# An attention and two-layer MLP kernel on one core: first transfers in the order of use, and a new written order of the first group's work

## The chip, the core and the metric

One core of a Trainium2 chip runs the whole kernel. The metric is the device time of one execution in microseconds (us); lower is better. The core has five engines that run side by side, each with its own queue in program order: the Tensor engine (PE in the profile, its weight loads PEld), the Vector engine (DVE), the Scalar engine (ACT), GpSimd (POOL) and SyncE (SP), which here does nothing but issue transfers.

## The reference

Three stages in a row. The first is an attention over 32 learned slots; batch 4, 8 heads, 576 tokens, head width 64:

```python
a = softmax(phi, axis=tokens)                      # per head and slot
k_m = a.T @ k;  v_m = a.T @ v                      # 32 x 64 per head
attn = softmax(q @ k_m.T / 8, axis=slots)
x = (attn @ v_m)                                   # 2304 tokens x 512
h = x @ w_in;  x2 = max(0.01 * h, h) @ w_out       # 512 -> 2048 -> 512
# then: each token goes to the best two of 8 experts, 512 -> 1024 -> 512
```

The change touches the first two lines of work alone: how batch 0 and batch 1 of the attention and the first 512 columns of the two-layer MLP get started.

## The kernel before, in words

**Groups and slots.** The MLP runs in groups (batch, chunk c of 512 of the 2048 middle columns). A group has 8 slots: two token halves u of 288 tokens, times four blocks f of 128 middle columns. A slot n is a middle product (six matmuls, L587) with its leaky maximum, and an output product (four column blocks of three matmuls, L625) that accumulates in PSUM over the four f of a half. From slot 8 on a loop plans the work. The first group (slots 0 to 7, batch 0, chunk 0), together with all that must precede it, is written out by hand, as one string of 221 step names (L1038 to L1049), each of which issues its instructions on every engine's queue in that order; this string is one of the two places that the change rewrites.

**The steps' names.** A digit behind a name is a batch, a half, a block or a slot.
- `mx`, `mt`, `mb`, `sb`, `ex`, `su`: phi of a batch: maximum over tokens (DVE, L331), its two transposes (PE, L338 and L346), subtraction (DVE, L352), exp (ACT, L356), sum (DVE, L361). `mx10` is batch 1, first half.
- `kk`, `kv`, `kb`: slot sums of k alone, v alone (batch 0) and both (batch 1) on PE (L379); `de`, `rd`, `no`, `kt`: denominator, reciprocal, normalizing on ACT (L399), transpose.
- `qa`, `qb`, `qc`: transposes of q (PE L368, ACT copy L370) for batch 0 first half, batch 0 second half, batch 1 first half. The steps beginning with `sa`, `sb`, `sc` are the softmax of the scores of the same three: scores (PE L416), transpose, maximum, subtraction, exp (ACT L436), sum, product, transpose back, and the split into a high and a low part (L457, L462).
- `c0` to `c7` with `a`, `h`, `s`, `l`, `o`: turning one 128 x 512 tile of 64-bit weights into 32-bit ones: one ACT pass (L204), three DVE passes (L210, L215, L220), and for tiles of the second layer (c4 to c7) the split into two parts (ACT L238, POOL L239). c0 to c3 are the first layer's tiles.
- `v0m`, `v0h`, `v0l`: v_m times the first layer's weights (PE L552) and its split (ACT L557, DVE L561). Every middle product needs all of it.
- `l0` to `l7` with `mm`, `sc`, `mx`, `hi`, `lo`: a slot's middle product (PE), scaled copy (ACT L593), maximum (DVE L598), split (ACT L603, POOL L608). `y20` is the output product of slot 2, column block 0.
- `Lqb`, `Lph`, `Lr6` and so on issue transfers.

**Buffers.** phi has one buffer; PSUM has four tiles of kind "y" (used by the start and by output products), two of kind "m", two of kind "h" (middle products).

**First transfers.** Before the string, SP issues phi, k of batch 0, two first-layer tiles, q, a third tile, v, the fourth tile and two tiles of the second layer (L255 to L273).

Of the kernel before, what the change touches and what calls it, by code (L numbers as in the profile page):

```python
# [20 lines left out]
def moe_kernel(  # L21
# [36 lines left out]
    NW, NRAW, NPOOL = 29, 4, 64  # L58
# [22 lines left out]
    def spare(s0, n, p=128):  # L81
        return big[:p, s0 * NDB * TU:s0 * NDB * TU + n]
# [85 lines left out]
    def load_q(b, u):  # L168
        if (b, u) == (1, 0):
            t = spare(2, HJ * H * D, P).rearrange("p (j h d) -> p j h d", j=HJ, h=H)  # L170
        else:
            t = att.tile([P, HJ, H, D], F32, name="q", bufs=1)
        for j in range(HJ):
            nc.sync.dma_start(t[:, j], q[b].rearrange("h (p j) d -> p j h d", j=J)[:, u * HJ + j])  # L174
        QR[b, u] = t
# [10 lines left out]
    def load_raw(n):  # L186
        if n >= len(items):
            return
        kind, a, db = items[n]
        if n in (NRAW, NRAW + 1):  # L190
            t = spare(6, 2048).bitcast(I32)[:, (n - NRAW) * 1024:(n - NRAW + 1) * 1024].rearrange("p (c t) -> p c t", t=2)
        else:
            t = conv.tile([128, 512, 2], I32, name="raw64", bufs=NRAW)
        if kind == "i":
            nc.sync.dma_start(t, w_in_w[db * 128:(db + 1) * 128, a * 512:(a + 1) * 512, :])  # L195
        else:
            nc.sync.dma_start(t, w_out_w[a * 128:(a + 1) * 128])
        RAW[n] = t
# [57 lines left out]
    kv0 = spare(0, 2 * H * J * D, P).rearrange("p (i h j d) -> p i h j d", i=2, h=H, j=J)  # L256
# [3 lines left out]
    def load_kv0(i):  # L260
        for s in range(2):
            nc.sync.dma_start(kv0[:, i, 4 * s:4 * s + 4].rearrange("p h j d -> p h (j d)"),
                              (k, v)[i][0, 4 * s:4 * s + 4].rearrange("h (p j) d -> p h (j d)", j=J))

    load_kv0(0)
    load_raw(0)
    load_raw(1)
    load_q(0, 0)
    load_raw(2)
    load_kv0(1)  # L270
    load_raw(3)
    load_raw(4)
    load_raw(5)  # L273


    jp = consts.tile([128, 128], I32)
# [759 lines left out]
    for c in range(3):  # L1036
        steps[f"Lk{c}"] = (load_kv, 1, c)
    order = """  # L1038
        mx00 mt00 mb00 mx01 sb00 ex00 mt01 mb01 sb01 ex01 kk0 su01 c1a kk1 kk2 su00 c1h dek c0a qa0 rdk nok qa1 qa2 ktk c1s
        c0h samm c2a Lqb c0s c0l Lr6 c2h kv0 kv1 kv2 Lph satr samx c4a c3a sasb saex c2s c2l nov qb0 qb1 ktv  # L1040
        c4h c1l Lr7 c3h c1o sasu c5a qb2 c3s samu sabk c2o sahi salo@g Lqc c0o v0m0 v0m1 c5h c5s mx10 c6a
        c3l c6h c5l mx11 c3o v0m2 v0m3 mt1 v0h0 v0l0 sbmm v0h1 v0l1 l0mm mb1 l1mm l0sc Lr8 sb10 ex10 sbtr c4s
        sb11 c4l c4o l1sc c7a sbmx l0mx l0hi l0lo sbsb qc0 l2mm l1mx l3mm y00 y01 c6s Lk0 c5o c7h l1hi l1lo sbex
        sbsu sbmu ex11 qc1 qc2 y02 l2sc l2mx l2hi y03 sbbk sbhi c6l su10 y10 y11 Lk1 Lk2 y12 kb0 kb1 kb2
        su11 deb l2lo Lr9 l3sc y13 c6o y20 l3mx l3hi l3lo y21 c7s c7l c7o y22 y23 sblo l4mm l5mm rdb nob
        l4sc l4mx l4hi l5sc l5mx l4lo y30 y31 ktb l6mm l6sc l6mx Lr10 y32 y33 scmm sctr y40 scmx y41 y42 y43
        l7mm l5hi l5lo v1m0 v1m1 v1m2 v1m3 Lr11 y50 y51 l7sc y52 scsb scex l6hi l7mx l7hi scsu scmu scbk
        schi l6lo sclo v1h0 y53 y60 l7lo v1h1 y61 y62 v1l0 y63 y70 y71 y72 v1l1 y73 Lqd
    """.split()  # L1049
    first = {"kk0", "kv0", "ktk", "ktv", "qa0", "qa1", "qa2", "samm", "v0m0", "mt00", "mt01", "mt1"}  # L1050
    engines = {"d": nc.vector, "g": nc.gpsimd}
# [227 lines left out]
```

## Time and profile before

| | us |
|---|---|
| median of 3 runs (921.24 to 923.18) | 921.34 |
| the profiled execution | 923.07 |
| its span, first to last instruction | 921.1 |
| PE busy in the span | 876.2 (95%) |
| DVE busy in the span | 544.0 (59%) |
| ACT busy | 355.9 (39%) |
| POOL busy | 194.3 (21%) |

The profiled execution is 1.73 us above the median, and 1.97 us of it lie around the span. Shares over the whole span are averages of stages with different limits, so the stage that the change touches (roughly the first 80 us) has to be read by itself: in the tables by stretch of time, in the list of who waited for whom, and in the instructions in order of time.

### The profile page before, as it was taken

The page shows a single profiled execution, that of the slowest core. Times are in us where ns is not written, and L with a number is a line of the kernel's source. Part 1 is how long each engine was busy: PE and PEld are TensorE (multiplying, and loading weights), DVE is VectorE, ACT ScalarE, POOL GpSimd, SP SyncE. Part 2 cuts the span into 40 slices and gives each one's busy share as a digit, 9 for nine tenths or more (in the row PEclk, how much of TensorE's full clock was granted, in tenths as well). Part 3 has the DMA queues.
Part 4 walks back from the last instruction along what each step waited for, and adds up shares of the span by engine and source line. Part 5 has one row for each costly group of instructions (what it writes and reads, how often), then busy time and mean ns, then how long its engine had stood idle before and what let it go on. Part 6 is the DMA issues. An engine that isn't in the chain of part 4 may idle for free.

```text
span 921.1 us, 16145 instructions
## 1 busy us (share of the span) xinstructions
PE 876.2 (95%) x6296; PEld 783.4 (85%) x6296; DVE 544.0 (59%) x1306; ACT 355.9 (39%) x784; POOL 194.3 (21%) x195
## 2 busy tenths in 40 slices
PE   4579999999999999999999999999999999999996
PEld 2377778999999998889888988998889888998895
DVE  5698988466666867878956544535444353442312
ACT  2346556545444544444624342333323332331110
POOL 0042224333200000000103320513215142130402
PEclk9999999999999999999999999999999999999998
DMA  8989723012431111212625543533434343230201
GB/s 208 256 178 192 187 73 93 1 46 74 172 145 46 35 59 50 75 43 82 203 78 186 186 148 114 190 104 129 145 113 169 125 146 139 98 122 1 82 22 57
DMA packets 82614, 105.29 MB, mean 114 GB/s; under 512 B 23988, under 2 KB 58836, under 8 KB 82528
## 3 DMA queue, kind: packets, MB, share of 16 engines
q1 hardware_dynamic: 70528, 71.58, 27.0%
q0 software_dynamic: 9312, 27.88, 9.1%
q10 hardware_dynamic: 2688, 4.72, 1.6%
q8 instruction: 51, 0.84, 0.4%
q14 instruction: 35, 0.29, 0.1%
HBM read 85.88 MB, written 19.53 MB: 114 GB/s over the span
## 4 chain that ended last, share of the span: by engine, by line
PE 82%; DVE 9%; DMA 3%; ACT 2%; SPq 2%; issue 1%; POOL 0%; POOLq 0%; DVEq 0%; ACTq 0%
PE py L881 24%; PE ph L863 23%; PE py L625 18%; PE ph L587 9%; PE pxt L838 2%; PE pvw L552 2%; PE pi L769 1%; DMA big<-in_moe_w_out_dram 1%; DMA row<-x,get 1%; DVE mx L361 1%; DVE wi L215 1%; SPq L195 1%; DVE mx L331 1%; SPq L174 1%; PE pg L653 1%
## 5 line engine op out<-in xcount | busy, mean ns | idle before, releaser
L863 PE MATMUL ph<-xh,w2l 128*128 128x256 f32 (+1 forms) x512 | 155.9, 305 | 0.0
L863 PE MATMUL ph<-xh,w2h 128*128 128x256 f32 (+1 forms) x512 | 155.7, 304 | 0.2 <-ACT xh L840 0.2
L625 PE MATMUL py<-gh,woh 128*128 128x288 f32 x512 | 154.8, 303 | 0.8 <-ACT big L632 0.6
L813 DVE TENSOR_TENSOR w2l<-r,w2h 128x512 fp32r<-128x512 f32 x128 | 87.6, 686 | 114.8 <-ACT w2h L812 54.0
L863 PE MATMUL ph<-xl,w2h 128*128 128x256 f32 (+1 forms) x512 | 155.3, 303 | 0.0
L625 PE MATMUL py<-gl,woh 128*128 128x288 f32 x512 | 153.1, 299 | 0.4 <-POOL gl L608 0.4
L625 PE MATMUL py<-gh,wol 128*128 128x288 f32 x512 | 151.6, 296 | 0.0
L881 PE MATMUL py<-w2h,gh 128*128 128x512 f32 (+1 forms) x320 | 129.4, 404 | 0.0
L812 ACT ACTIVATE w2h<-r 128x512 fp32r<-128x512 f32 x128 | 79.5, 628 | 123.3 <-PE py L881 94.1
L881 PE MATMUL py<-w2h,gl 128*128 128x512 f32 (+1 forms) x320 | 126.3, 395 | 0.0
L866 ACT ACTIVATE gh<-ph 128x256 fp32r<-128x256 f32 (+1 forms) x128 | 54.4, 425 | 186.1 <-PE ph L863 173.7
L881 PE MATMUL py<-w2l,gh 128*128 128x512 f32 (+1 forms) x320 | 126.2, 395 | 0.0
L867 DVE SCALAR_TENSOR_TENSOR gl<-ph,gh 128x256 fp32r<-128x256 f32 (+1 forms) x128 | 60.5, 473 | 99.9 <-ACT gh L866 92.6
L825 POOL DMA_INDIRECT row<-x,get x40 | 43.9, 1096 | 345.4 <-DVE put L776 228.6
L625 PEld LDWEIGHTS py<-gh,woh 128*128 128x128 f32 x512 | 96.5, 189 | 18.1 <-issue 15.7
L863 PEld LDWEIGHTS ph<-xh,w2h 128*128 128x128 f32 x512 | 96.5, 189 | 5.0 <-ACT xh L840 0.7
L625 PEld LDWEIGHTS py<-gl,woh 128*128 128x128 f32 x512 | 96.6, 189 | 3.6 <-issue 2.7
L863 PEld LDWEIGHTS ph<-xl,w2h 128*128 128x128 f32 x512 | 96.5, 188 | 3.3 <-DVE xl L841 0.2
L625 PEld LDWEIGHTS py<-gh,wol 128*128 128x128 f32 x512 | 96.8, 189 | 0.5 <-issue 0.5
L863 PEld LDWEIGHTS ph<-xh,w2l 128*128 128x128 f32 x512 | 96.4, 188 | 0.0
L598 DVE TENSOR_TENSOR sm<-ph,sm 128x288 f32<-128x288 f32 x128 | 57.5, 451 | 57.5 <-ACT sm L593 56.8
L608 POOL TENSOR_TENSOR gl<-sm,gh 128x288 fp32r<-128x288 f32 x64 | 59.2, 927 | 127.0 <-ACT gh L603 111.3
(164 smaller groups left out, 1507.8 us busy)
## 6 DMA issues: line engine op xcount, KB each, us to landing
r<-in_moe_w_dram SPq DMA_DIRECT2D x64, 512.0 KB, 3.7
raw<-in_moe_w_in_dram SPq DMA_DIRECT2D x16, 512.0 KB, 3.9
raw<-in_moe_w_out_dram SPq DMA_DIRECT2D x14, 512.0 KB, 4.2
out_dram<-zr SPq DMA_DIRECT2D x18, 256.0 KB, 3.0
x<-xr ACTq DMA_DIRECT2D x24, 192.0 KB, 2.1
q<-in_q_dram SPq DMA_DIRECT2D x21, 192.0 KB, 4.9
phi<-in_phi_dram SPq DMA_DIRECT2D x8, 288.0 KB, 3.1
kv<-in_k_dram SPq DMA_DIRECT2D x6, 384.0 KB, 6.3
```

The lines of the kernel that those rows point to most:

```text
L552: nc.tensor.matmul(VW[b, c][g][hp * M:(hp + 1) * M, :], VT[b][g * 64:(g + 1) * 64, 1, hp * M:(hp + 1) * M], WI[c, hp][g * 64:(g + 1) * 64, ...
L587: nc.tensor.matmul(ph, w_[:, o:o + 128], a_[:, g], start=(t == 0), stop=(t == 5))
L598: nc.vector.tensor_tensor(sm, ph, sm, op=OP.max)
L608: (eng or (nc.gpsimd if n < NPOOL else nc.vector)).tensor_sub(lo, sm, hi.bitcast(F32))
L625: nc.tensor.matmul(py, w_[:, s], g_, start=(first and i == 0), stop=(last and i == 2))
L812: nc.scalar.activation(h_, src, AF.Copy)
L813: nc.vector.tensor_sub(l_, src, h_.bitcast(F32))
L825: nc.gpsimd.indirect_dma_start(out=xg[:sz], out_offset=None, in_=x2[:(B - 1) * S] if (e, c) == (0, 0) else x2, in_offset=bass.IndirectOffs ...
L863: nc.tensor.matmul(ph[:, :n], w_[:, s], x_[:, db], start=(t == 0), stop=(t == 3 * NDB - 1))
L866: nc.scalar.activation(hi, ph[:, :n], AF.Relu)
L867: nc.vector.scalar_tensor_tensor(lo, ph[:, :n], 0.0, hi.bitcast(F32), op0=OP.max, op1=OP.subtract)
L881: nc.tensor.matmul(PY[c, t][:sz], h_[:, o:o + sz], w_, start=(f == 0 and i == 0), stop=(f == NF2 - 1 and i == 2))
```

## The change

It does two things. SP's first transfers come in another order: q ahead of the first weight tile, v right behind that tile, and the other tiles after v. And the string of steps is written anew: the same 221 names, none added or taken out. Output products stand right behind the middle products of their slots, the conversion of the second layer's tiles stands between them, and the work on phi of batch 1 (`mx10`, `mx11`, `mt1`, ...) stands behind the conversion of the last tile.

```diff
     load_kv0(0)
+    load_q(0, 0)
     load_raw(0)
-    load_raw(1)
-    load_q(0, 0)
-    load_raw(2)
     load_kv0(1)
-    load_raw(3)
-    load_raw(4)
-    load_raw(5)
+    for n in range(1, NRAW + 2):
+        load_raw(n)
...
-        c4h c1l Lr7 c3h c1o sasu c5a qb2 c3s samu sabk c2o sahi salo@g Lqc c0o v0m0 v0m1 c5h c5s mx10 c6a
...
+        sbex l2mx l2hi l2lo l3mm y00 y01 y02 y03 c6a c6h Lr8 l3sc l3mx l3hi l3lo sbsu sbmu c6s c6l c6o sbbk sbhi sblo
```

SP's queue, where the program starts; before:

```order
L151 DMA phi<-in_phi_dram 96x4x192 x2
L262 DMA big<-in_k_dram 96x4x384 x2
L195 DMA raw_87<-in_moe_w_in_dram 128x1024
L195 DMA raw_89<-in_moe_w_in_dram 128x1024
L174 DMA q<-in_q_dram 96x8x64 x3
L195 DMA raw_95<-in_moe_w_in_dram 128x1024
L262 DMA big<-in_v_dram 96x4x384 x2
L195 DMA raw_99<-in_moe_w_in_dram 128x1024
```

and with the change:

```order
L151 DMA phi<-in_phi_dram 96x4x192 x2
L262 DMA big<-in_k_dram 96x4x384 x2
L174 DMA q<-in_q_dram 96x8x64 x3
L195 DMA raw_91<-in_moe_w_in_dram 128x1024
L262 DMA big<-in_v_dram 96x4x384 x2
L195 DMA raw_95<-in_moe_w_in_dram 128x1024
L195 DMA raw_97<-in_moe_w_in_dram 128x1024
L195 DMA raw_99<-in_moe_w_in_dram 128x1024
```

v has moved ahead of three weight tiles; q has moved ahead of all.

DVE's queue around the first middle products, from the back transpose of the first softmax on; before (`mx<-phi` is the maximum over batch 1's phi, `vwl` the last thing that the middle products wait for):

```order
L451 STREAM_TRANSPOSE ar<-sx 128x576
L210 TENSOR_SCALAR wi<-wi 128x512
L215 SCALAR_TENSOR_TENSOR wi<-big,wi 128x512
L331 TENSOR_REDUCE mx<-phi 96x128
L220 SCALAR_TENSOR_TENSOR wi<-raw_99,wi 128x512
L210 TENSOR_SCALAR wi<-wi 128x512
L220 SCALAR_TENSOR_TENSOR wi<-big,wi 128x512
L331 TENSOR_REDUCE mx<-phi 96x128
L340 TENSOR_REDUCE cm<-pm 128x2
L561 TENSOR_TENSOR vwl<-pvw,vwh 128x512 x2
```

and with the change (line numbers are lower by three from here on):

```order
L448 STREAM_TRANSPOSE ar<-sx 128x576
L220 SCALAR_TENSOR_TENSOR wi<-raw_95,wi 128x512
L210 TENSOR_SCALAR wi<-wi 128x512
L215 SCALAR_TENSOR_TENSOR wi<-raw_97,wi 128x512
L220 SCALAR_TENSOR_TENSOR wi<-raw_97,wi 128x512
L210 TENSOR_SCALAR wi<-wi 128x512
L215 SCALAR_TENSOR_TENSOR wi<-raw_99,wi 128x512
L220 SCALAR_TENSOR_TENSOR wi<-raw_99,wi 128x512
L558 TENSOR_TENSOR vwl<-pvw,vwh 128x512 x2
```

Both maxima, the reduction of their transposes and five passes over second-layer tiles no longer stand ahead of `vwl`.

DVE's queue where those maxima now stand, behind the last pass over tile 7 (`raw_319`; `sm` is a slot's maximum, `ups` to `cnt` are constants for later):

```order
L220 SCALAR_TENSOR_TENSOR wi<-raw_319,wi 128x512
L328 TENSOR_REDUCE mx<-phi 96x128
L293 TENSOR_SCALAR ups<-jp 96x96
...
L595 TENSOR_TENSOR sm<-ph,sm 128x288
L328 TENSOR_REDUCE mx<-phi 96x128
...
L595 TENSOR_TENSOR sm<-ph,sm 128x288
L337 TENSOR_REDUCE cm<-pm 128x2
L349 TENSOR_TENSOR phi<-phi,pm 96x768 x2
L595 TENSOR_TENSOR sm<-ph,sm 128x288
L358 TENSOR_REDUCE mx<-phi 96x128 x2
L595 TENSOR_TENSOR sm<-ph,sm 128x288
```

From here on batch 1's maxima, subtractions and sums follow one another, with one slot maximum between them at a time.

## Rows read from the trace of the kernel before

**Rows 1.** Busy time of each engine by stretch; behind a stretch its length, (x) instructions.

```profile
0.00:22.60 22.60, 9.63 (x133) 6.57 (x133) 11.38 (x19) 6.80 (x12) 1.67 (x8) 1.00 0.85 207
22.60:43.60 21.00, 11.30 (x144) 5.78 (x144) 14.60 (x26) 6.61 (x14) 1.41 (x1) 1.00 1.05 259
43.60:81.80 38.20, 32.47 (x306) 28.72 (x299) 32.45 (x53) 18.12 (x43) 14.55 (x14) 1.00 0.95 197
81.80:155.00 73.20, 68.77 (x723) 59.33 (x722) 68.43 (x118) 45.19 (x105) 18.82 (x20) 1.00 0.49 123
155.00:438.00 283.00, 281.22 (x2225) 260.95 (x2224) 196.02 (x624) 131.64 (x308) 33.97 (x37) 1.00 0.21 70
```

**Rows 2.** In order of time: start, us, engine, line; in brackets idle before it.

```profile
12.97 2.78 PE L379 MATMUL pk<-big,phi 96*32 96x64 f32 x92 [2.06 <-DMA big<-in_k_dram]
...
26.88 2.78 PE L379 MATMUL pk<-big,phi 96*32 96x64 f32 x92 [2.24 <-DMA big<-in_v_dram]
...
37.69 1.44 DVE L331 TENSOR_REDUCE mx<-phi 96x128 f32<-96x768 f32 x1 [1.75 <-DMA phi<-in_phi_dram]
...
39.78 1.92 PE L552 MATMUL pvw<-wi,kvT 64*32 64x512 f32 x4 [3.50 <-DVE wi L220]
...
43.59 0.61 PE L587 MATMUL ph<-ah,vwh 128*128 128x288 f32 x1
...
80.52 1.28 DVE L561 TENSOR_TENSOR vwl<-pvw,vwh 128x512 fp32r<-128x512 f32 x2
```

**Rows 3.** DVE's waits, 43.6 to 81.8: in total, times, longest.

```profile
DVE sm L598 <- ACT sm L593: 2.7, 4, 0.8
DVE phi L352 <- PE pm L346: 1.8, 1, 1.8
```

**Rows 4.** By stretch, as rows 1; the last two columns are DMA share and GB/s.

```profile
15.50:19.50 4.00, 3.01 (x25) 2.57 (x17) 1.59 (x5) 2.11 (x6) 0.00 (x0) 1.00 0.49 119
19.50:30.00 10.50, 5.12 (x117) 3.33 (x115) 5.60 (x10) 2.65 (x7) 0.00 (x0) 1.00 1.08 298
```

**Rows 5.** By stretch, instructions on the softmax's tile sx alone: DVE busy, ACT busy.

```profile
22.50:34.40 11.90, 4.62 (x7) 0.67 (x1) 1.00 1.05 296
```

**Rows 6.** DVE in order of time: three conversion passes, and the softmax's start.

```profile
22.59 0.84 DVE L423 STREAM_TRANSPOSE sx<-psc 128x288 f32<-128x288 f32 x2
...
34.78 0.43 DVE L210 TENSOR_SCALAR wi<-wi 128x512 int32<-128x512 int32 x1 [0.46 <-ACT wi L204]
35.24 0.69 DVE L215 SCALAR_TENSOR_TENSOR wi<-big,wi 128x512 int32<-128x512 int32 x1
...
39.98 0.68 DVE L220 SCALAR_TENSOR_TENSOR wi<-big,wi 128x512 int32<-128x512 int32 x1
```

**Rows 7.** Groups of 0 to 85: busy us, mean ns, then idle before.

```profile
L370 ACT ACTIVATE qT<-pq 128x384 f32<-128x384 f32 x12 | 5.7, 495 | 3.9 <-PE pq L368 3.7
L204 ACT ACTIVATE wi<-raw 128x512 f32<-128x512 f32 x8 | 5.3, 671 | 8.0 <-DMA raw<-in_moe_w_in_dram 7.0 <-DMA raw<-in_moe_w_out_dram 1.0
L603 ACT ACTIVATE gh<-sm 128x288 fp32r<-128x288 f32 x9 | 3.9, 447 | 5.2 <-DVE sm L598 5.2
L593 ACT ACTIVATE sm<-ph 128x288 f32<-128x288 f32 x9 | 3.7, 411 | 5.1 <-PE ph L587 5.0
L238 ACT ACTIVATE woh<-wi 128x512 fp32r<-128x512 f32 x4 | 2.5, 631 | 3.7 <-DVE wi L220 3.7
```

**Rows 8.** PE in order of time, products of the same size (288 columns).

```profile
53.73 0.45 PE L625 MATMUL py<-gh,woh 128*128 128x288 f32 x1
53.98 0.45 PE L625 MATMUL py<-gl,woh 128*128 128x288 f32 x1
...
56.48 0.29 PE L625 MATMUL py<-gl,woh 128*128 128x288 f32 x1
56.60 0.29 PE L625 MATMUL py<-gh,wol 128*128 128x288 f32 x1
```

**Rows 9.** SP in order of time: phi of batch 2, issued once its buffer is free.

```profile
62.33 0.33 SPq L151 DMA_DIRECT2D phi<-in_phi_dram  x1
```

More of the change, by code (lines that the diff above doesn't have):

```diff
@@ L1038, in moe_kernel @@
     order = """
-        mx00 mt00 mb00 mx01 sb00 ex00 mt01 mb01 sb01 ex01 kk0 su01 c1a kk1 kk2 su00 c1h dek c0a qa0 rdk nok qa1 qa2 ktk c1s
-        c0h samm c2a Lqb c0s c0l Lr6 c2h kv0 kv1 kv2 Lph satr samx c4a c3a sasb saex c2s c2l nov qb0 qb1 ktv
-        c4h c1l Lr7 c3h c1o sasu c5a qb2 c3s samu sabk c2o sahi salo@g Lqc c0o v0m0 v0m1 c5h c5s mx10 c6a
[L1042 to L1048, printed above, removed]
+        mx00 mt00 mb00 mx01 sb00 ex00 mt01 mb01 sb01 ex01 kk0 su00 kk1 kk2 su01 dek qa0 c0a rdk nok qa1 qa2 ktk c0h c0s
+        c0l Lqb samm Lr6 satr samx c1a sasb saex kv0 kv1 kv2 Lph c1h c1s nov sasu c2a samu ktv sabk c1l Lr7 c2h c2s sahi
+        c0o c1o salo@g c3a c2l Lqc c3h c3s c3l c2o c3o v0m0 v0m1 v0m2 v0m3 v0h0 v0l0 v0h1 v0l1 c4a c4h qb0 qb1 l0mm
+        l1mm c4s l0sc c4l qb2 l0mx c4o l0hi l0lo c5a sbmm c5h l1sc c5s l1mx l1hi l1lo l2mm sbtr c5l c5o l2sc sbmx sbsb
+        sbex l2mx l2hi l2lo l3mm y00 y01 y02 y03 c6a c6h Lr8 l3sc l3mx l3hi l3lo sbsu sbmu c6s c6l c6o sbbk sbhi sblo
+        y10 y11 y12 y13 c7a c7h Lk0 c7s c7l c7o qc0 Lr9 y20 y21 y22 y23 l4mm l4sc mx10 l4mx l4hi l4lo qc1 qc2 Lk1 Lk2 l5mm
+        mx11 l5sc l5mx l5hi l5lo y30 y31 y32 y33 mt1 mb1 sb10 ex10 l6mm l6sc sb11 l6mx ex11 l6hi l6lo su10 Lr10
+        y40 y41 y42 y43 kb0 kb1 kb2 su11 deb l7mm l7sc l7mx l7hi l7lo rdb nob y50 y51 y52 ktb scmm sctr y53 scmx
+        y60 y61 Lr11 v1m0 v1m1 v1m2 v1m3 scsb scex y62 y63 v1h0 v1h1 scsu y70 v1l0 scmu scbk y71 schi v1l1 sclo y72 y73 Lqd
     """.split()
```

## The prediction

> **What bounds the kernel now.** I read the busy time by stretch first. From 155 us on PE is full (281.22 of the 283.00 us of the last stretch) and DVE is not; between 81.8 and 155 us both are close to full, 68.77 and 68.43 of 73.20 us [rows 1]. Nothing in those stretches is edited, so whatever the change does, it does by moving the moment at which slot 8 can start. That moment is 81.8 us, the end of the split of batch 1's v product: DVE's two instructions from 80.52 us [rows 2]. A shift of it goes through to the end, because the work behind it fills DVE and then PE and leaves no slack to take it up.
>
> So the first 81.8 us are the case. Here DVE is the fullest engine: 11.38, 14.60 and 32.45 us in the three stretches, together 58.43 us of work [rows 1]. The other 23.4 us it waits: 11.2 us up to 22.6, 6.4 us up to the first middle product at 43.59, and 5.75 us from there. The string names the same steps before and after, so DVE's 58.4 us stay. **The forecast is therefore a count of DVE's waits in the new order.**
>
> **Up to the first softmax.** The new transfer order closes a hole: between 15.5 and 19.5 us the DMA engines worked at a share of 0.49, against 1.08 right after [rows 4], that is (1.08 - 0.49) / 1.08 x 4 = 2.2 us of lost transfer. Batch 0's v, needed at 26.88 us before [rows 2], gets those 2.2 us and the time of two tiles of 0.52 MB that no longer precede it, 3.5 us at 298 GB/s [rows 4]: it should land at about 21 us. I cost this at nothing, and say what hides it. The slot sums of v take 2.9 us on PE [rows 2] and are ready long before DVE is: DVE begins the softmax at 22.59 us [rows 6]. That start hangs on k (used at 12.97, unmoved [rows 2]), on PE's transposes and on ACT's copies, which stand in nearly the old order; I take 22.2 us, since one conversion pass (0.43 us [rows 6]) less stands ahead. The cover is gone only if v came after about 28 us.
>
> **From there to the first middle product.** DVE's row is now nearly gapless: the softmax 4.62 us on its tile [rows 5] and 0.45 us for the reciprocal, three conversions of 0.43 + 0.69 + 0.68 = 1.8 us each [rows 6], 5.4 together. That gives 22.2 + 4.6 + 0.45 + 5.4 = 32.7; with 0.8 us for short waits and the overlap with POOL, 33.5. In the kernel before, the last v product began at 39.78 and the first middle product at 43.59, 3.8 us later [rows 2]; so the first middle product now comes at **37.3 us, 6.3 us earlier**. DVE waits 2.6 us of these 3.8 (the product of 1.92 us [rows 2], then ACT's copy).
>
> That head start is not a gain by itself. By 43.59 us DVE had before also done batch 1's two maxima (2 x 1.44 us [rows 2]) and five passes over second-layer tiles (0.43 + 0.43 + 0.69 + 0.43 + 0.68 = 2.66 [rows 6]): 5.5 us that are still ahead in the new order. On DVE's account the lead is 6.3 - 5.5 = 0.8 us. What decides is how much DVE waits from here.
>
> **From the first middle product to slot 8.** Before, DVE waited 5.75 us of 38.2, mostly for ACT's scaled copies and once for PE [rows 1, 3]. In the new order I go along the queues with the durations of [rows 7]:
> - The pass over tile 5 waits for ACT. In ACT's queue stand, after the third q transpose, its copy 0.50, the high part of tile 4 0.63, slot 0's high part 0.45, and tile 5's first pass 0.67: 2.25 us. That q transpose stands behind two middle products on PE, which at the slow spacing (below) take 1.45 us each: 37.3 + 2.9 + 0.9 = 41.1, plus 2.25 = 43.3 us. DVE has nothing before it but tile 4's passes and slot 0's maximum, until 39.7. **3.5 us.**
> - Tile 6's pass waits likewise behind the exp of the second softmax 0.67 [rows 5], a high part 0.45 and ACT's pass 0.67, while DVE has one maximum of 0.45: **1.4 us.**
> - Batch 1's phi: its transposes need two PSUM tiles of kind "y", which ACT frees by copying slot 3's output, one copy after the other behind slot 5's high part (0.45); then PE, reduction, PE again before the subtraction can go. Five hand-overs, of which DVE fills only its own: **2.1 us.**
> - Slot 7's maximum stands behind batch 1's sums on PE: the denominator, six products at 0.13 us [rows 8], ACT's copy 0.41 and four hand-overs: **2.1 us.** The scores of batch 1 wait for normalizing, transpose, copy and product, 2.8 us less the 1.5 us maximum of batch 2 that DVE has to do: **1.3 us.**
> - Exps and high parts under which DVE has nothing else: 0.8, 0.8, 0.2; slot maxima that wait for ACT's copy: 0.45, 0.5, 0.4. **3.15 us.**
>
> Sum 13.55 us, against 5.75 before. The cause is one: before, batch 1's phi, conversions and the second softmax were spread among one another, so that each hid the others' hand-overs; now conversions come first and batch 1 comes last, as a chain with little beside it.
>
> **The sum.** Waits 11.2 + 2.6 + 13.55 + 0.25 (small gaps) = 27.6 us; with 58.4 us of work slot 8 starts at 86.0 us, against 81.8: **4.2 us later**. The profiled execution would take 927.3 us instead of 923.07; the median moves from 921.34 to **925.5 us**. The uncertain terms are the waits: none of the five items can be below 0 (that side, 13.55 us less, gives 912) and each was counted as if nothing else of the later program came into the hole. Above, doubling the two that hang on PE's speed (3.5 and 2.1) gives 931.
>
> Now the clock. Products of 288 columns start 0.25 us apart at 53.7 us and 0.12 to 0.13 us apart at 56.5 [rows 8]: the lower of TensorE's two levels (1.2 GHz), then the higher (2.4 GHz), after a stretch in which PE hardly paused; later waits before 81.8 us did not bring the lower one back. The Trainium skill (TensorE: Matmul & The Clock Gate, section Why this matters for your kernels) speaks against the change here: it asks for no idle gaps between bursts, since PE otherwise falls back to the lower level. The row of slot 2's output products in the new order would have such a gap of some 4 us, in front of the split of tile 6. By that page the time would come out at the second rival's 928; by the rows alone I stay at 925.5.
>
> **The rivals.** A difference of 0.2% (1.84 us) is about what a measurement of this kernel can tell from no change.
> 1. *Faster: the lead survives.* If from the first middle product to slot 8 the new order needs no more than the old 38.2 us, slot 8 starts at 75.5 and the time is 915. Then DVE may wait 3.3 us there in all. For it: PE, ACT and POOL are far from full there (32.47, 18.12, 14.55 of 38.20 [rows 1]). Against it: the waits are hand-overs, not load. It decides at a sum of waits behind the first product of 7.5 us, where 13.55 are counted. Chance 0.17.
> 2. *Slower still: PE at the lower level again, late.* Products of slots 4 to 7 then take 1.45 instead of 0.8 us; four of them stand in batch 1's chain, 2.6 us: 928.1. Against it: no fall in the kernel before. Or phi of batch 2, whose one buffer was free at 62.33 [rows 9], gets it only behind batch 1's sums, some 11 us later, and its maximum stands ahead of the scores in DVE's queue: the 2 to 3 us of that transfer would show there, 928 as well. Chance 0.15.
> 3. *No difference.* Waits between 7.5 and 11.2 us behind the first product: 921 to 923. This is also where it ends if the transfers are all that takes effect, since nothing waits for them last. Chance 0.13.
> 4. *The forecast,* 924 to 927: 0.55.
>
> **How the numbers follow.** Slower by over 0.2%: 0.55 + 0.15 = 0.70. Within: 0.13. Faster: 0.17. The range takes half of rival 1 (917, halfway from no change to its price and a little beyond) and rival 2 with the doubled waits (931).
>
> **What would show it.** Right: first middle product at 36 to 39 us; v's slot sums at 21 to 23 us; in DVE's waits the first pass of a conversion on ACT's pass (L210 on L204) late, around 43 and 49 us; slot 8's products starting at 85 to 88 us; DVE busy 58 to 60 us until then; everything behind unchanged in length. Wrong: the products of slot 8 before 80 us, or DVE's waits behind the first product under 7.5 us. If slot 8 starts late but the end does not move, the stretch behind it had slack, and my step from slot 8 to the end was the wrong one.

## The result and the profile after

The changed kernel takes 928.96 us (median of 4 runs, 928.07 to 931.92) against 921.59 us for the kernel before (4 runs, 921.24 to 923.18): 1.0087 times, 95% interval 1.0073 to 1.0101, that is 7.4 us slower. The profiled execution took 929.69 us, its span is 927.8 us (921.1 before), its mean granted clock 0.988 (0.997 before).

The busy time by stretch, in stretches that answer to those of [rows 1]. Behind the length of a stretch stand PE, its weight loads, DVE, ACT and POOL, then the granted TensorE clock (1.00 for 2.4 GHz, 0.50 for 1.2 GHz), the DMA share and GB/s:

```profile
0.00:22.60 22.60, 9.95 (x137) 6.74 (x137) 12.40 (x19) 5.45 (x10) 1.67 (x8) 1.00 0.93 218
22.60:36.30 13.70, 11.11 (x117) 4.14 (x117) 9.03 (x16) 4.50 (x10) 1.40 (x1) 1.00 0.93 286
36.30:85.30 49.00, 35.25 (x330) 28.84 (x328) 39.16 (x65) 23.88 (x55) 13.82 (x14) 0.91 0.92 183
85.30:161.80 76.50, 71.81 (x713) 61.72 (x714) 66.34 (x115) 43.69 (x101) 20.41 (x21) 0.95 0.48 118
161.80:444.80 283.00, 281.23 (x2226) 260.97 (x2225) 195.74 (x623) 131.44 (x307) 33.37 (x37) 1.00 0.20 69
```

The last row is that of before to 0.01 us of PE: from 161.8 us on everything is what it was, 6.8 us later. The row above it is not. In the kernel before DVE waited 73.20 - 68.43 = 4.8 us in that stretch [rows 1], here 76.50 - 66.34 = 10.2 us, and PE's clock, 1.00 in every stretch of [rows 1], is 0.95 there and 0.91 in the row above. (The clock column tells of falls, not of the start: it reads 1.00 before the first rise too, where [rows 8] show products 0.25 us apart.)

PE in order of time, the marks of the prediction:

```profile
22.81 2.77 PE L376 MATMUL pk<-big,phi 96*32 96x64 f32 x92 [2.24 <-DMA big<-in_v_dram]
...
36.30 0.40 PE L584 MATMUL ph<-ah,vwh 128*128 128x288 f32 x1
...
53.88 0.61 PE L622 MATMUL py<-gh,woh 128*128 128x288 f32 x1 [3.99 <-ACT woh L238]
...
79.85 0.29 PE L622 MATMUL py<-gh,wol 128*128 128x288 f32 x1
81.56 0.55 PE L365 MATMUL pq<-ident,q 96*128 96x96 f32 x4 [1.41 <-DVE vwl L558]
82.69 0.72 PE L365 MATMUL pq<-ident,q 96*128 96x96 f32 x4 [0.58 <-ACT qT L367]
83.61 0.90 PE L365 MATMUL pq<-ident,q 96*128 96x96 f32 x4 [0.20 <-DVE vwl L558]
84.22 0.83 PE L584 MATMUL ph<-ah,vwh 128*128 128x288 f32 x2
85.34 0.61 PE L584 MATMUL ph<-al,vwh 128*128 128x288 f32 x1 [0.29 <-DVE al L459]
...
88.14 0.44 PE L584 MATMUL ph<-al,vwh 128*128 128x288 f32 x1
88.38 0.44 PE L584 MATMUL ph<-ah,vwl 128*128 128x288 f32 x1
```

The first middle product comes at 36.30 us (43.59 before [rows 2]), slot 2's output products wait 3.99 us for tile 6, slot 8 begins at 84.22 us (80.35 before). Behind that, products of 288 columns stand 0.24 us apart, where before they stood 0.12 to 0.13 apart from 56 us on [rows 8]. The same trace, divided where the granted clock changes:

```profile
36.00:52.20 16.20, 9.70 (x78) 7.79 (x75) 12.99 (x22) 8.36 (x19) 6.47 (x6) 1.00 1.19 234
52.20:59.00 6.80, 4.61 (x17) 4.26 (x18) 5.95 (x9) 2.89 (x5) 1.95 (x2) 0.50 0.84 160
59.00:82.90 23.90, 19.30 (x232) 15.74 (x232) 17.87 (x32) 10.53 (x26) 5.40 (x7) 1.00 0.73 156
82.90:89.80 6.90, 6.41 (x39) 4.58 (x38) 5.74 (x12) 3.19 (x8) 0.00 (x0) 0.51 1.13 215
89.80:100.00 10.20, 8.56 (x139) 7.49 (x139) 9.41 (x15) 6.12 (x12) 2.40 (x3) 1.00 0.53 138
100.00:103.40 3.40, 3.40 (x16) 3.40 (x16) 1.37 (x5) 1.37 (x4) 0.81 (x1) 0.50 0.76 191
```

PE reaches the higher level (2.4 GHz) 20 us earlier than before (at 35.2 instead of 55.3 us), and falls back to 1.2 GHz three times: inside the gap of 3.99 us, amid the waits between 80.15 and 83.61 us ahead of slot 8, and behind a wait of 1.08 us for batch 2's sums. In the two later stretches PE is busy nearly all the time (6.41 of 6.90, 3.40 of 3.40 us). What DVE waits for there, in order of time:

```profile
88.44 0.41 ACT L590 ACTIVATE sm<-ph 128x288 f32<-128x288 f32 x1 [2.76 <-PE ph L584]
88.89 0.46 DVE L595 TENSOR_TENSOR sm<-ph,sm 128x288 f32<-128x288 f32 x1 [0.86 <-ACT sm L590]
...
100.17 0.44 PE L622 MATMUL py<-gh,woh 128*128 128x288 f32 x1
...
103.05 0.44 PE L584 MATMUL ph<-ah,vwh 128*128 128x288 f32 x1
...
104.94 0.46 DVE L595 TENSOR_TENSOR sm<-ph,sm 128x288 f32<-128x288 f32 x1 [3.58 <-ACT sm L590]
```

A slot's maximum on DVE waits for ACT's scaled copy, and that for PE's middle product. The longest wait of DVE behind slot 8, 3.58 us, is for a middle product that stands on PE behind twelve output products 0.24 us apart. Of the 10.2 us that DVE waits behind 85.3 us, 1.1 lie before 89.8 us and 3.6 between 100 and 106 us.

DVE in order of time, its first softmax and then, up to the last input of slot 8, the instructions that waited and some that took long:

```profile
20.31 0.85 DVE L420 STREAM_TRANSPOSE sx<-psc 128x288 f32<-128x288 f32 x2 [0.77 <-PE psc L413]
...
24.80 0.43 DVE L210 TENSOR_SCALAR wi<-wi 128x512 int32<-128x512 int32 x1 [2.07 <-ACT wi L204]
...
41.13 0.72 DVE L210 TENSOR_SCALAR wi<-wi 128x512 int32<-128x512 int32 x1 [1.40 <-ACT wi L204]
41.88 1.16 DVE L215 SCALAR_TENSOR_TENSOR wi<-big,wi 128x512 int32<-128x512 int32 x1
...
48.43 0.58 DVE L210 TENSOR_SCALAR wi<-wi 128x512 int32<-128x512 int32 x1 [1.28 <-ACT wi L204]
...
63.65 0.36 DVE L337 TENSOR_REDUCE cm<-pm 128x2 f32<-128x192 f32 x1 [1.25 <-PE pm L335]
64.52 1.82 DVE L349 TENSOR_TENSOR phi<-phi,pm 96x768 f32<-96x768 f32 x2 [0.51 <-PE pm L343]
...
72.02 0.46 DVE L595 TENSOR_TENSOR sm<-ph,sm 128x288 f32<-128x288 f32 x1 [2.01 <-ACT sm L590]
...
73.29 1.49 DVE L328 TENSOR_REDUCE mx<-phi 96x128 f32<-96x768 f32 x1 [0.54 <-DMA phi<-in_phi_dram]
75.24 0.85 DVE L420 STREAM_TRANSPOSE sx<-psc 128x288 f32<-128x288 f32 x2 [0.46 <-PE psc L413]
...
83.48 0.41 DVE L210 TENSOR_SCALAR wi<-wi 128x512 int32<-128x512 int32 x1
83.92 0.69 DVE L215 SCALAR_TENSOR_TENSOR wi<-raw,wi 128x512 int32<-128x512 int32 x1
84.53 0.75 DVE L459 TENSOR_TENSOR al<-ar,ah 128x576 fp32r<-128x576 f32 x1
```

### The profile page after: what moved, and what is told of

Read it like the earlier page. It is cut to its first block, busy times and chain, and to the rows that moved or that the text cites. A ratio compares the mean times of both kernels' runs of the same rounds, so it can differ in the third digit from the quotient of the medians.

```text
span 927.8 us, 16159 instructions
## 1 busy us (share of the span) xinstructions
PE 882.3 (95%) x6296; PEld 784.5 (85%) x6296; DVE 543.8 (59%) x1306; ACT 356.8 (38%) x784; POOL 195.3 (21%) x195
## 4 chain that ended last, share of the span: by engine, by line
PE 80%; DVE 7%; issue 5%; DMA 3%; POOL 2%; ACT 2%; SPq 1%; POOLq 0%; DVEq 0%; ACTq 0%
PE py L878 24%; PE ph L860 23%; PE py L622 17%; PE ph L584 9%; PE pvw L549 2%; PE pxt L835 2%; POOL gl L605 1%; DMA row<-x,get 1%; DVE wi L215 1%; DMA raw<-in_moe_w_in_dram 1%; PE pi L766 1%; DVE wi L220 1%; PE pg L650 1%; SPq L174 1%; PE px L665 1%
```

## The experiments

The table reads the profiled executions against the kernel before's: how much later (+) or earlier (-) than there the first middle product of slots 0, 8 and 30 starts (43.59, 80.35 and 160.11 us there), how much this shift grows from slot 8 to slot 30, and how long the granted clock was at 1.2 GHz from 80 us to slot 30. Ratios are of timed runs, each to runs of the kernel before on the same chip, with 95% intervals. A name with _again is the same program run a second time (phi_later_again that of phi_later_only).

| kernel | ratio | slot 0 | slot 8 | slot 30 | growth | at 1.2 GHz |
|---|---|---|---|---|---|---|
| changed | 1.0087 (1.0073 to 1.0101) | -7.3 | +3.9 | +6.8 | 2.9 | 10.2 |
| changed_again | 1.0083 (1.0064 to 1.0101) | -8.8 | +2.5 | +5.4 | 2.9 | 10.2 |
| transfers_only | 1.0018 (1.0009 to 1.0027) | -0.9 | 0.0 | +0.4 | 0.4 | 3.4 |
| string_only | 1.0098 (1.0077 to 1.0118) | -7.6 | +3.1 | +5.1 | 2.0 | 6.8 |
| outputs_only | 1.0024 (1.0011 to 1.0038) | -2.0 | -0.7 | +0.5 | 1.2 | 6.8 |
| phi_later_only | 1.0087 (1.0068 to 1.0106) | -7.1 | -0.1 | +3.8 | 3.9 | 10.2 |
| phi_later_again | 1.0066 (1.0045 to 1.0086) | -2.1 | +4.2 | +5.7 | 1.5 | 10.2 |
| phi_later_fill | 1.0059 (1.0040 to 1.0078) | -3.8 | +4.4 | +3.8 | -0.6 | 0 |
| fill_early | 1.0095 (1.0075 to 1.0115) | -7.7 | +4.0 | +7.0 | 3.0 | 10.2 |
| fill_both | 1.0058 (1.0043 to 1.0073) | -7.2 | +4.5 | +3.7 | -0.8 | 0 |
| fill_late_8 | 1.0066 (1.0048 to 1.0084) | -8.3 | +2.6 | +2.8 | 0.2 | 0 |
| fill_late_8_again | 1.0079 (1.0061 to 1.0097) | -7.6 | +3.1 | +4.8 | 1.7 | 6.8 |
| tile6_first | 1.0101 (1.0080 to 1.0122) | -9.1 | +2.9 | +5.8 | 2.9 | 10.2 |
| woven_2 | 0.9986 (0.9974 to 0.9997) | -7.3 | -4.3 | -4.3 | 0.0 | 0 |
| woven_3 | 0.9982 (0.9968 to 0.9996) | -8.8 | -3.9 | -5.7 | -1.8 | 0 |
| woven_3_old_transfers | 1.0006 (0.9992 to 1.0019) | -7.8 | -1.4 | +0.2 | 1.6 | 3.4 |

The profiled execution of the kernel before is one of its slower ones (923.07 us; its medians beside these kernels are 920.65 to 921.88), so a shift in the table looks better by 1 to 2.4 us than the times do.

**Which part of the change.** Three kernels take one part each.

transfers_only: the kernel before with the first part of the change alone, the new order of `load_kv0`, `load_q` and `load_raw`; the string stays the old one.

> The kernel before with the new order of first transfers alone, the old order of steps kept. Theory A (the loss comes from the order of steps, the transfers alone are worth little): tile 1 now lands behind v, near 23.5 us instead of 17.2, while its first pass stands early in ACT's old queue, ahead of q's copies, so the first softmax starts 4 to 6 us later; v comes earlier and gives some of it back; first middle product at 45 to 46 us instead of 43.6, end 0 to 2 us later than the kernel before (921.5 to 923.5). Theory B (the transfers carry the loss): 4 us or more slower than the kernel before.

922.37 us, 1.7 us slower. Theory A holds for the softmax: ACT waits 12.2 us for tile 1 and the softmax begins at 27.63 us instead of 22.59 [rows 6]. But the first middle product does not come later, as expected, it comes at 42.72 us. From its softmax to there DVE waits 0.75 us in all, where it waited 6.4 in the kernel before, for ACT's first passes over tiles and for phi; v's sums are not earlier (27.48 us, 26.88 before [rows 2]).

string_only: the new string with the old first transfers.

> The changed order of steps with the old order of first transfers. Theory A: the order of steps carries the whole loss and the late v adds to it: first middle product near 39 us instead of 36.3, end 2 to 3 us later than the changed kernel (930 to 932). Theory B (the transfers carry the loss): the time falls back to within 1 us of the kernel before.

929.08 us, first middle product at 36.02. Theory A in kind: the string carries the whole loss. But the first middle product was expected near 39 us and the end at 930 to 932: the later v did not delay the one, and the ratio (1.0098 against 1.0087, intervals overlapping) shows no cost of the old transfers to the new string that is clear of noise.

outputs_only: the kernel before with the output products in one piece, for each of slots 0 to 4 as here.

```diff
...
-        sb11 c4l c4o l1sc c7a sbmx l0mx l0hi l0lo sbsb qc0 l2mm l1mx l3mm y00 y01 c6s Lk0 c5o c7h l1hi l1lo sbex
-        sbsu sbmu ex11 qc1 qc2 y02 l2sc l2mx l2hi y03 sbbk sbhi c6l su10 y10 y11 Lk1 Lk2 y12 kb0 kb1 kb2
+        c7a sbmx l0mx l0hi l0lo sbsb qc0 l2mm l1mx l3mm y00 y01 y02 y03 c6s Lk0 c5o c7h l1hi l1lo sbex sbsu sbmu ex11
+        qc1 qc2 l2sc l2mx l2hi sbbk sbhi c6l su10 y10 y11 y12 y13 Lk1 Lk2 kb0 kb1 kb2 su11 deb l2lo Lr9 l3sc c6o y20
...
```

> The kernel before, with the output products of slots 0 to 4 alone written in one piece, each group of four right behind one another, instead of split up by other steps. Theory A (batch 1's phi carries the loss): within 2 us of the kernel before, 919 to 923. Theory B (the output products carry it): 924 or more.

923.61 us: 1.7 us slower, between Theory A's 923 and Theory B's 924, and about a quarter of the whole change's loss.

phi_later_only: in the kernel before, batch 1's phi moved behind slot 4.

```diff
-        c4h c1l Lr7 c3h c1o sasu c5a qb2 c3s samu sabk c2o sahi salo@g Lqc c0o v0m0 v0m1 c5h c5s mx10 c6a
-        c3l c6h c5l mx11 c3o v0m2 v0m3 mt1 v0h0 v0l0 sbmm v0h1 v0l1 l0mm mb1 l1mm l0sc Lr8 sb10 ex10 sbtr c4s
+        c4h c1l Lr7 c3h c1o sasu c5a qb2 c3s samu sabk c2o sahi salo@g Lqc c0o v0m0 v0m1 c5h c5s c6a c3l c6h c5l c3o
...
+        l4mx l4hi mx11 l5sc l5mx l4lo y30 y31 y32 y33 mt1 mb1 sb10 ex10 l6mm l6sc sb11 l6mx ex11 l6hi su10 l6lo Lr10
+        y40 y41 y42 y43 kb0 kb1 kb2 su11 deb l7mm l5hi l5lo Lr11 l7sc l7mx l7hi rdb nob y50 y51 y52 ktb scmm sctr scmx
```

> The kernel before, its transfers and its order, with batch 1's phi steps alone (maxima, transposes, subtraction, exps, sums, k/v sums, normalizing, transpose) moved behind slot 4, to the places between the slots where the changed kernel has them. Theory A (batch 1's phi as a chain at the end, with nothing beside it, is the part that costs): slot 8 3 to 5 us later than in the kernel before, and 0 to 3 us more if PE's clock falls at slot 8: 924 to 929. Theory B (that part is harmless and the loss comes from output products right behind the middle layer): within 1.5 us of the kernel before.

927.67 us. This one part costs as much as the whole change (0.87%; 0.66% in its repeat). Where it costs was only half as expected: in this profile slot 8 is on time (-0.1) and all of the 3.8 us comes behind it; in the repeat slot 8 is 4.2 us late. In both, PE stands still 4.1 us ahead of slot 8 and falls to 1.2 GHz there. It also gives a head start by itself (slot 0 at -7.1; -2.1 in the repeat): in the kernel before, batch 1's first maximum stands ahead of the first middle product and waits 1.75 us for phi [rows 2].

**PE's clock.** A step `again` issues products whose result nobody reads, to hold PE busy across a gap:

```diff
+    def again(k):
+        ph = psum.tile([128, TU], F32, name="ph", tag="h", bufs=2)
+        for _ in range(k):
+            nc.tensor.matmul(ph, VW[0, 0, 0][0][:, 0:128], AT[0, 0][0][:, 0], start=True, stop=True)
...
+        sbhi sblo y10 y11 y12 y13 c7a c7h Lk0 c7s c7l c7o qc0 Lr9 f28 y20 y21 y22 y23 l4mm l4sc mx10 l4mx l4hi l4lo
...
+        sclo y72 y73 f16 Lqd
```

fill_early has `f28` alone, fill_both both, fill_late_8 an `f8` in the place of `f16` alone.

> The changed kernel with 28 extra products of 288 columns on PE (0.13 us each, 3.7 us) in the gap of 3.99 us ahead of slot 2's output products; their result is not used. Theory A (PE's fall to 1.2 GHz follows the gap): no fall at 52.2 us, products of slots 2 to 5 at 0.13 us spacing, slot 4's first product up to 2 us earlier; because DVE is busy 5.95 of the 6.8 us at the lower level, the end moves by 0 to 1.5 us only. Theory B (the gap has nothing to do with it): the granted clock still falls near 52 us and the time stays within 0.5 us of the changed kernel.

929.96 us. The clock did stay up over 52 us (it fell at 42.3 instead), slot 4 began 1.65 us earlier, and at slot 8 nothing of it was left (+4.0, as against +3.9). So filling the gap gained nothing. What a fall costs there is not shown by it: PE spent as long at 1.2 GHz ahead of slot 8 as without the filling (6.8 us, here 42.3 to 49.2).

> As the run before, with 16 more such products (2.1 us) behind slot 7's output products, where PE idles at 79.98 to 81.56 us and 82.1 to 82.7. The automatic order behind that place changes a little with it. Theory A (the 2.9 us that are lost behind the start of slot 8 are the two stretches at 1.2 GHz, 82.9 to 89.8 and 100.0 to 103.4): the clock stays at 2.4 GHz from 35 us on and the time is 2 to 4 us below the changed kernel, 925 to 927. Theory B (they come from the order in which slots 8 to 12 stand against the batch 2 work): clock up, time within 1 us of the changed kernel.

926.29 us, and no fall from 67.8 us on. The shift does not grow behind slot 8. The order behind slot 8, which the loop plans and the string does not fix, is another one here, so this alone does not separate the theories.

> The changed kernel with 8 products of 288 columns (1.06 us, their result not used) behind slot 7's output products, so that PE's idle 1.41 us there shrinks to some 0.4; every other instruction on PE, DVE and ACT keeps the order of the changed kernel as far as slot 20. Theory A (the loss behind slot 8's start is PE at 1.2 GHz): the granted clock stays up from 59 us on, the shift against the kernel before stays at 3.9 to 4.5 us from slot 8 on and the time falls by 2 to 3 us against the changed kernel, to 926 to 927. Theory B (the order of slots 8 to 12 against batch 2's work makes that loss): clock up, but slot 9's output products still come 10 us later than in the kernel before, and the time stays within 1 us of the changed kernel.

925.92 us; no fall from 58 us on, and the shift stays at 2.6 to 2.8. Slot 9's output products do come 8.3 us late, in the order of the changed kernel, and by slot 30 the shift of 2.8 is all that is left of it. So that order as a whole costs next to nothing here. In its repeat the clock fell all the same:

> The run with 8 unused products behind slot 7, repeated beside the changed kernel itself. Theory A (PE's fall to 1.2 GHz at slot 8 carries 2.9 us of the loss): 2 to 3.5 us below the changed kernel of this call. Theory B (the difference seen before was between chips): within 1 us of it.

927.14 us, 1.0 us under the changed kernel run beside it (928.14), the intervals overlapping: by the times neither theory is decided. The two profiles decide more than the times do, for they are one program on one chip. The stretch behind slot 8's start, in fill_late_8 and in its repeat:

```profile
83.60:90.40 6.80, 5.58 (x51) 4.54 (x52) 6.56 (x12) 3.80 (x10) 0.79 (x1) 1.00 1.04 224
```

```profile
83.60:90.40 6.80, 6.12 (x38) 4.57 (x37) 5.68 (x11) 2.75 (x7) 0.09 (x1) 0.50 1.07 228
```

At 2.4 GHz PE ran 51 products and DVE was busy 6.56 of 6.80 us; at 1.2 GHz 38 products and 5.68 us, and the shift grew by 1.7 us instead of 0.2. The price can be followed in two waits. From the last input of slot 8 (`al`) on, DVE has the same 32 instructions in the same order in fill_late_8, its repeat and the changed kernel. Two slot maxima among them, in fill_late_8:

```profile
86.69 0.46 DVE L595 TENSOR_TENSOR sm<-ph,sm 128x288 f32<-128x288 f32 x1
...
100.94 0.46 DVE L595 TENSOR_TENSOR sm<-ph,sm 128x288 f32<-128x288 f32 x1 [2.05 <-ACT sm L590]
```

and in the repeat:

```profile
88.36 0.46 DVE L595 TENSOR_TENSOR sm<-ph,sm 128x288 f32<-128x288 f32 x1 [0.86 <-ACT sm L590]
...
102.94 0.46 DVE L595 TENSOR_TENSOR sm<-ph,sm 128x288 f32<-128x288 f32 x1 [2.05 <-ACT sm L590]
```

The changed kernel, at 1.2 GHz ahead of both, waits 0.86 and 3.58 us. So the first wait is there only behind the first fall, and the second fall makes the second wait 1.5 us longer; the other 2.05 us belong to the order of steps. The growths, 0.2, 1.7 and 2.9 us, go with it. Over the whole table growth follows the time at 1.2 GHz: -1.8 to 0.2 us where there is none, 0.4 to 1.6 with 3.4 us of it, 1.2 to 2.0 with 6.8, 1.5 to 3.9 with 10.2. It is not the clock alone: phi_later_only and its repeat, one program, both have 10.2 us of it and grow by 3.9 and 1.5.

> The changed kernel as it is, on the same chip as the next run, so that the two can be compared directly. Every theory: 1.007 to 1.010 times the kernel before, the granted clock at the lower level in two or three stretches behind 50 us.

928.14 us, three falls behind 50 us, as in the first profile.

> The run with batch 1's phi steps alone moved behind slot 4, repeated beside the next one so that the two can be compared directly. Every theory: 1.007 to 1.010 times the kernel before; slot 8 starts within 1 us of the kernel before, and the loss of some 4 us of its profile builds up behind it, with two or three falls of the granted clock.

> The same with 28 products of 288 columns (3.7 us, their result not used) behind slot 7's output products, where PE waits 4.14 us for the high part of batch 1's v product; every other instruction on PE, DVE and ACT keeps its order as far as slot 20. Theory A (the loss behind slot 8 is PE at 1.2 GHz after that gap): no fall at 80 us and at most one behind it, the shift behind slot 8 stays within 0 to 1.5 us, and the time is 2.5 to 5 us below the run beside it. Theory B (the loss behind slot 8 comes from the order in which DVE and ACT do that stretch's work): the clock holds, and the time stays within 1 us of the run beside it.

```diff
-        v1l1 y73 Lqd
+        v1l1 y73 f28 Lqd
```

phi_later_again 928.38 us, phi_later_fill 926.60. The first took 1.0066 times the kernel before and its slot 8 came 4.2 us late, neither as expected. With the gap filled no fall comes behind 59.8 us, and the shift goes from 4.4 to 3.8 us instead of from 4.2 to 5.7. Behind slot 8 that is Theory A's profile. In the times the step is 1.8 us, less than expected and with overlapping intervals; and the order behind slot 8 did differ by some instructions, contrary to what the expectation says.

**The gap at tile 6.** The second softmax's sums and multiplication behind tile 6's passes:

```diff
-        sbex l2mx l2hi l2lo l3mm y00 y01 y02 y03 c6a c6h Lr8 l3sc l3mx l3hi l3lo sbsu sbmu c6s c6l c6o sbbk sbhi sblo
+        sbmx sbsb sbex l2mx l2hi l2lo l3mm y00 y01 y02 y03 c6a c6h Lr8 l3sc l3mx l3hi l3lo c6s c6l c6o sbsu sbmu sbbk
```

> The changed kernel with the second softmax's sums and multiplication (2.45 us of DVE) written behind tile 6's passes instead of ahead of them. Theory A (slot 2's output products and PE's gap of 3.99 us hang on that order): the split of tile 6 is ready some 2.5 us earlier, PE's gap shrinks to 1 to 2 us, no fall of the clock at 52 us; since DVE's work is only exchanged, slot 8 starts within 1 us of the changed kernel and the end with it, 926 to 929. Theory B (the gap is a cause of the loss itself): the end moves by the whole 2.5 us.

928.54 us. The gap shrinks from 3.99 to 2.07 us, slot 2's output products begin 4 us earlier, and the end does not move: Theory A, except that the clock fell all the same (at 41.1 and 51.4 us).

**Keeping the lead.** Two strings with the changed kernel's transfers and head; only behind `qb1` the steps stand in another order, in which DVE has something to do in each wait. A piece of woven_3:

```diff
-        l1mm c4s l0sc c4l qb2 l0mx c4o l0hi l0lo c5a sbmm c5h l1sc c5s l1mx l1hi l1lo l2mm sbtr c5l c5o l2sc sbmx sbsb
+        qb1 c4s c7a l0mm c4l c7h l0sc qb2 c5a c6a l0mx sbmm l0hi c7s l1mm c4o c5h l0lo c6h sbtr l1sc sbmx Lr8 sbsb qc0
...
-        y40 y41 y42 y43 kb0 kb1 kb2 su11 deb l7mm l7sc l7mx l7hi l7lo rdb nob y50 y51 y52 ktb scmm sctr y53 scmx
+        y30 Lk1 mb1 l4hi l5mx l4lo Lk2 y12 sb10 sb11 l6mm ex10 l7mm y11 ex11 kb0 kb1 su10 l5hi su11 l5lo kb2 deb l6sc
```

> The changed kernel, transfers and the string up to the transposes qb1 as changed (the head start), and behind that the same steps in another order: batch 1's phi, conversions, slots and the second softmax mixed so that DVE always finds a step whose inputs are there, found by adding up the traces' durations along the queues. Theory A (the lead of 7 us at the first middle product is lost in waits of DVE, not in work): DVE's waits from there to slot 8 fall from about 10 us to 2 to 5, slot 8 starts at 75 to 80 us, and the time is 914 to 921, under the kernel before. Theory B (the lead is lost to something else, for instance transfers or PE's clock): slot 8 no earlier than 82 us and the time at or above the kernel before.

> As the run before with another such order (batch 1's maxima at the place where the changed kernel has them, its later steps earlier). Theory A: slot 8 at 75 to 80 us, time 914 to 921. Theory B: slot 8 no earlier than 82 us, time at or above the kernel before.

918.98 and 918.61 us: both faster than the kernel before, by 0.14% and 0.18%, with intervals that leave out no change. In woven_3, from its first middle product to slot 8, and behind it:

```profile
34.83:76.44 41.61, 34.74 (x322) 27.70 (x320) 36.18 (x62) 21.61 (x50) 13.85 (x14) 0.92 0.98 198
76.44:154.42 77.98, 75.11 (x772) 64.09 (x770) 69.27 (x121) 48.29 (x114) 23.93 (x23) 1.00 0.51 126
```

DVE waits 41.61 - 36.18 = 5.4 us up to slot 8 (4.5 in woven_2), where the changed kernel has 9.8, and PE runs its output products up to slot 8's start; the clock is 1.00 behind it. woven_2 has batch 1's maxima early (the first ahead of `l0mm`), woven_3 about where the changed kernel has them; both win. So a late place of batch 1's phi does not by itself cost the time. That the chain with little beside it does is the reading that fits phi_later_only and both of these; it is not shown apart, since the two orders move conversions and output products too.

woven_3_old_transfers is woven_3 with the first transfers of the kernel before.

> The second woven order with the first transfers of the kernel before. Theory A (the new transfers give the head start that the woven order keeps): first middle product near 39 us instead of 35, slot 8 1 to 4 us later than with the new transfers, time 919 to 922. Theory B (the gain of the woven order has nothing to do with the transfers): 918 to 919, as with the new ones.

921.24 us. Against the kernel before that is 1.0006 where woven_3 has 0.9982, some 2.2 us more, with intervals that overlap slightly. Slot 8 comes 2.5 us later, as Theory A said; the first middle product, in these two profiles, only 0.9. Its profile also has a fall of the clock (at 123.9 us) that woven_3's has not. So the new transfers seem to be worth some 2 us to a string that keeps the lead, while the old string (transfers_only) loses 1.7 us by them.

## Why the prediction was right in sign and short in size

**Up to the first middle product: right.** The first softmax began at 20.31 us instead of the 22.2 counted, the first middle product came at 36.30 instead of 37.3; v's sums began on PE at 22.81, between 21 and 23 as said, and nothing on DVE waited for v. One thing was overlooked: DVE's row behind the softmax's start is not nearly gapless, it waits 2.07 us (at 24.80) for ACT's pass over tile 1, which now comes behind v. DVE's waits up to 36.30 us are 14.9 us, where 13.8 were counted.

**From there to slot 8: the sum right, two terms wrong.** The last input of slot 8, DVE's low part of the scores' split (`al`), was ready at 85.28 us; 86.0 was forecast, 81.80 us was the time before (by the split of batch 1's v product, which is ready at 83.56 now). So this part of the loss is 3.5 us, forecast 4.2. Slot 8's first product, forecast for 85 to 88 us, began at 84.22, since it needs only the high part. The waits were over-sized: 9.8 us where 13.8 were counted (13.55 and 0.25). In the trace the pass over tile 5 waits 1.40 us (3.5 counted), that over tile 6 1.28 (1.4), slot 7's maximum 2.01 (2.1), phi's two hand-overs 1.25 and 0.51 (2.1), the scores 0.46 and the phi of batch 2 ahead of them 0.54 (1.3). Tile 5 was over-sized in the main because the middle products were priced at the lower level of the clock, 1.45 us each; PE had been at 2.4 GHz since 35.2 us. Against it DVE had 39.1 us of work there where 34.9 were left to it: at 36.30 it had done 12.40 + 9.03 = 21.4 us instead of 23.5, it took in 1.1 us of a later tile's passes (at 83.48 and 83.92), and some passes ran long (1.16 us at 41.88, where 0.69 was counted). The two errors cancel, which was luck. Of the rivals' sums one is off: waits of 7.5 to 11.2 us give, by the prediction's own addition, 919.5 to 923.2 us for "no difference", not 921 to 923.

**From slot 8 to the end: this step failed.** "A shift of it goes through to the end, because the work behind it fills DVE and then PE and leaves no slack to take it up." No slack to take a delay up does not mean that nothing is added. PE had run out of work at 80.15 us, worked 1.9 us of the next 4.1, and slots 8 to 12 then ran in part at 1.2 GHz. DVE waited 10.2 us in the stretch that was to be "unchanged in length", instead of 4.8, 4.4 of them in the two waits for middle products shown above, and the shift grew from 3.9 to 6.8 us: 2.9 us that the prediction had put at nothing. The rest to the 7.4 us of the medians is within the spread of the executions.

The prediction had the mechanism, as its second rival, in the wrong place. It looked for the fall at slot 2's gap, priced 2.6 us in batch 1's chain, and held against it that no wait in the kernel before had brought the lower level back. The gap came as foreseen (3.99 us) and the fall with it (52.2 us), but DVE was busy 5.95 of those 6.80 us and slot 8 began no later than counted. What that fall cost is not shown apart: fill_early and tile6_first moved it and had as much time at 1.2 GHz ahead of slot 8 (6.8 us). The clock fell again ahead of slot 8, where the prediction did not look, because PE's wait for slot 8 was read as DVE's affair. The section of the Trainium skill that was weighed there (TensorE: Matmul & The Clock Gate, Why this matters for your kernels) asks for no idle gaps between bursts; the trace agrees with it, at 0.50 granted clock after each of the three waits. What the runs add is that the price of a fall shows where DVE waits for PE (0.86 us and 1.5 us in the two waits followed above). The same page (HAM oscillation — how this bites in real kernels) counts half of the time at the lower level as lost. By that, as an estimate, the 10.2 us at slot 8 and behind it would cost 5.1; the growth was 2.9.

**What the runs leave open.** The profiles put some 3 us of the loss on the clock; the times of the filled kernels are only 1 to 3 us lower, with intervals that overlap or nearly do. Single executions point both ways: the one of fill_early's six with the highest mean clock (0.995) took 925.92 us, the others, at 0.986 to 0.990, 929.79 to 931.74; but the fastest of changed_again (926.46) had the lowest clock of its six (0.986). And the trace of the kernel before that all shifts are read against has a mean clock of 0.997, the highest of that kernel; its other executions, down to 0.990, must have had time at 1.2 GHz too (as an estimate, 0.007 x 921 x 2 = 13 us at most), no trace shows where, and were not clearly slower for it: at 0.997 it took 920.71 to 923.07 us, at 0.990 and 0.991 918.24 to 923.67. So how much of the 7.4 us between the medians is the clock stays open. Whether batch 1's late phi costs ahead of slot 8 or behind it differs from execution to execution.

## What to carry to other kernels

A head start in a hand-ordered stage is worth only what the next stage's waits leave of it: count the bottleneck engine's waits to the end of the stage, and spread a dependent chain among independent work before moving anything earlier. When a delay is passed on to a later stage, ask what the other engines do meanwhile: here a TensorE that worked 1.9 of 4.1 us began the next stage at half its clock, and that added to the delay where DVE waited for it. Judge an earlier transfer together with the order of steps that is to use it.

## What was not expected of the hardware

The same program fell to the lower level in one execution and not in another (fill_late_8 and its repeat, on one chip: mean clock 0.988 to 0.994 in the six executions of the one, 0.985 to 0.988 in those of the other), and the kernel before ranged from 917.5 to 923.7 us with mean clocks of 0.990 to 0.997. The Trainium skill (TensorE: Matmul & The Clock Gate, What's actually happening) calls the number of slow products at a kernel's start variable from run to run; these runs show the same of falls later on.

Transfers varied as much. In phi_later_only and its repeat, one program on two chips, ACT's wait for the same second-layer tile, up to 42 us, was

```profile
ACT wi L204 <- DMA big<-in_moe_w_out_dram: 6.4, 1, 6.4
```

```profile
ACT wi L204 <- DMA big<-in_moe_w_out_dram: 10.3, 1, 10.3
```

and the first middle product came at 36.51 in the one and at 41.46 us in the other, while the ends lie 1.9 us apart.
